# Finishing a two-step projection in the slot where it began, in an attention kernel paced by its exps

## The chip, the cores and the metric

One core of a Trainium2 chip. The metric is the device time of one execution in microseconds, the median over the runs of a kernel. Each run also records the mean clock that was granted to TensorE (1.000 is full speed). Ratios between kernels are the mean time of one kernel's fast runs over that of the other's fast runs of the same rounds, so they are not quite the ratio of the medians quoted beside them.

## The reference, cut to what matters

Two independent attention blocks on a sequence of 2048 with 32 heads of 16 columns, their outputs side by side:

```python
def _A_ref(x, wqkv, wo):          # every query sees every key
    ...
    p = _softmax(jnp.einsum("bhqd,bhkd->bhqk", q, k) * (Dh ** -0.5), axis=-1)
    o = jnp.einsum("bhqk,bhkd->bhqd", p, v)
    return (...o...) @ wo
def _B_ref(x, wqkv, wo):          # as A, with a causal window of 256
    mask = (idx[:, None] - idx[None, :] >= 0) & (idx[:, None] - idx[None, :] < W)
    ...
return jnp.concatenate([a, b], axis=-1)
```

Block A alone needs 32 x 2048 x 2048 exps. These set the time.

## The kernel before

The kernel is a scheduler. It cuts the work into 731 slots. A slot is one exp of up to three score tiles of 128 x 512 on ScalarE (some slots hold narrower ones, of block B, so that there are 747 exps), and round it the scheduler emits TensorE's work: scores of the slot after next, values of finished exps, and at the end of the slot at most a little other work. Two buffers of three PSUM banks hold scores ("sps"), one bank holds values ("op"), and a single bank ("ms") serves everything else: projections (k, q, v, output, and "padded" ones for the first heads), some guards, and a share of the exps that VectorE computes with a polynomial (steps "d").

A projection needs four matmuls. It is cut into two steps of two, and the bank is open between them:

```python
    def busy(self, bank, n):                       # warm-up: result never used
        for _ in range(n):
            self.nc.tensor.matmul(bank, lhsT=self.ident[:], rhs=self.junk, start=True, stop=True)
    ...
    def pair(self, first, second):
        def f():
            self.open = self.bank()
            first(self.open[:])                    # two matmuls
        def g():
            bank, self.open = self.open, None
            self.closed = self.slot
            second(bank[:])                        # two matmuls, then VectorE's copy
        return [f, g]
    ...
    def scores(self, slot):
        ...
            if b == 0 and jb.inst == 0:
                self.busy(sps[:, 0, :], 2 - self.whole)   # ahead of the scores
    ...
    def fill(self, s, tasks, done):
        if self.open is None:
            if self.closed == s or not self.by(self.freed, 0.9):
                return False
            ...                                    # pick the next task that may run
        ...
        self.whole += (kind in "kqop") * 2 + (kind in "dv")
        t["steps"].pop(0)()
        ...
    # end of each slot in run():
            self.whole = 0
            ...                                    # a guard or a step "d", if the bank is free
            must = self.open is not None           # a pair begun in the last slot
            while ((credit >= (CROWD if full else 1.0) or must)
                   and self.fill(s, tasks, done)):
                credit -= 1.0
                must = False
                if full:
                    break
```

`credit` grows with the urgency of the tasks; `CROWD` is 3.0. So a pair normally takes two slots, and one slot only if there was credit for two steps. `full` marks a slot whose coming scores all have a mask. `whole` counts how much work the slot gave to TensorE; a slot with less than 2 gets warm-up matmuls ("fillers" below) ahead of the next scores of block A.

Of the kernel before, what the change touches and what calls it, by code (L numbers as in the profile page):

```python
# [114 lines left out]
class _Kernel:  # L115
# [900 lines left out]
    def run(self):  # L1016
        done = set(self.start())
        self.vec = self.freed = self.op_free = 0.0
        slots, self.pend = self.slots()
        self.poly_pend = {key: list(groups) for key, groups in self.poly.items()}  # L1020
        tasks = self.plan(slots, done)
        polys = [t for t in tasks if t["name"][0] == "d"]
        tasks = self.tasks = [t for t in tasks if t["name"][0] != "d"]
        credit = poly_credit = 0.0
        for n in range(2):
            self.whole = n - 1
            self.scores(slots[n])
        self.whole = 2
        for s, sl in enumerate(slots):
            self.slot = s  # L1030
            self.exps(sl)
            if s == 2:
                self.more_constants()
                self.load_wo(0)
            if self.dq and self.by(self.vec, 0.6):
                self.queued(1.22, at=0)
                self.dq.pop(0)()
            if s + 2 < len(slots):
                self.scores(slots[s + 2])
            elif s + 1 == len(slots):  # L1040
                self.mid, finish = self.last_out(0, NPASS - 1)
            self.values()
            due = [x for x in self.later if x[0] <= s]
            self.later = [x for x in self.later if x[0] > s]
            for _, f in due:
                f()
            credit = min(credit + min(self.rate(s, tasks), 2.5), 3.0)
            poly_credit = min(poly_credit + self.rate(s, polys), 3.0)
            self.whole = 0
            if (self.guards and self.guards[0][0] <= s and self.open is None  # L1050
                    and self.by(self.freed, 0.9)):
                self.guards.pop(0)[1]()
                self.closed = s
                self.whole = 1
            full = s + 2 < len(slots) and all(jb.blocks for jb in slots[s + 2]["jobs"])
            if (poly_credit >= (2.5 if full else 1.0) and self.open is None
                    and self.fill(s, polys, done)):
                poly_credit -= 1.0
            must = self.open is not None
            while ((credit >= (CROWD if full else 1.0) or must)  # L1060
                   and self.fill(s, tasks, done)):
                credit -= 1.0
                must = False
                if full:
                    break
        while self.pend:
            self.slot += 1
            if self.dq:
                self.dq.pop(0)()
            self.values()  # L1070
            assert self.slot < len(slots) + 30, (self.dq, polys, self.poly_pend)
        assert not tasks + polys and not self.guards, [t["name"] for t in tasks]
        for _, f in sorted(self.later, key=lambda x: x[0]):
            f()
        finish()
# [49 lines left out]
```

## Time and profile before

| | before |
|---|---|
| median of the first 4 runs (the prediction starts from 1030.4, the median of the three known by then) | 1029.65 us (1028.13 to 1030.47) |
| ScalarE busy | 993.7 us, 97% of the span |
| TensorE busy | 918.5 us, 89% |
| wide exps (128 x 1536) | 705, 957.8 us |
| lateness of the wide exps | 25.2 us |
| fillers | 613 |

"Lateness" is used throughout. It is worked out from the trace: for each wide exp, the distance from the end of the exp before it to its own end, less 1.343 us, the distance that most of them keep; then summed. It is what ScalarE loses when scores come late. The lines that carry this are in the prediction.

### The profile page before, as it was taken

Reading aid. Unit: us, or ns where it says so; the run is one execution under the profiler, and the core shown is the slowest. Engines: PE = TensorE matmul, PEld = TensorE weight load, DVE = VectorE, ACT = ScalarE, POOL = GpSimd, SP = SyncE. Lnnn points to the kernel's source line nnn. Section 1 sums busy time; section 2 is a strip of 40 time slices with the busy share of each in tenths; the row PEclk is TensorE's granted clock in tenths of the full one; section 3 lists DMA queues with packets and bytes.
Section 4 is the critical chain, followed back from the end, with each engine's and each line's share of the span. In section 5 each row is a group of like instructions: output and inputs, shape, how many; then the busy total and the mean of one; then the engine's idle time right before and its main releaser. Section 6 shows DMA issues by size and latency. Waiting matters only on the chain.

```text
span 1027.8 us, 18725 instructions
## 1 busy us (share of the span) xinstructions
PE 918.5 (89%) x7577; PEld 314.1 (31%) x7658; DVE 804.2 (78%) x1032; ACT 993.7 (97%) x763; POOL 20.0 (2%) x100
## 2 busy tenths in 40 slices
PE   7999889899888998988899899899998998998887
PEld 5322222232223322332323332233332333233322
DVE  4532279887968898788888898988898878988874
ACT  5999999989999999999999999999999999999996
POOL 6000000000000000000000000000000000000000
PEclk9999999989999999999999999999999999999999
DMA  7021431212232102221240213123202221230011
GB/s 247 8 81 38 144 111 46 76 61 64 74 88 76 64 21 92 79 74 38 74 117 21 74 63 96 58 75 90 79 20 82 74 90 45 60 107 27 32 34 42
DMA packets 72359, 73.05 MB, mean 71 GB/s; under 512 B 22584, under 2 KB 55888, under 8 KB 72272
## 3 DMA queue, kind: packets, MB, share of 16 engines
q1 hardware_dynamic: 69216, 68.01, 21.4%
q0 software_dynamic: 768, 2.13, 0.5%
q10 hardware_dynamic: 2288, 1.70, 0.5%
q8 instruction: 60, 0.98, 0.4%
q14 instruction: 27, 0.22, 0.1%
HBM read 38.65 MB, written 31.07 MB: 68 GB/s over the span
## 4 chain that ended last, share of the span: by engine, by line
ACT 52%; PE 22%; DVE 14%; issue 10%; DMA 2%; ACTq 0%; DVEq 0%
ACT pT L599 52%; PE sps L572 5%; PE ms L252 4%; PE op L691 4%; PE sps L156 4%; DVE dy L631 3%; DVE dh L642 3%; DVE dh L646 2%; PE sps L581 2%; PE ms L628 2%; DVE pD L652 1%; DMA kTa<-in_A_x_dram 1%; DVE ob L421 1%; DVE osb L772 1%; DMA wk<-in_B_wqkv_dram 1%
## 5 line engine op out<-in xcount | busy, mean ns | idle before, releaser
L599 ACT ACTIVATE pT<-sps 128x1536 bf16<-128x1536 f32 (+2 forms) x747 | 983.6, 1465 | 15.4 <-PE sps L572 10.5
L156 PE MATMUL sps<-ident 128*128 128x512 bf16 x613 | 206.8, 382 | 46.6 <-ACT pT L599 39.1
L572 PE MATMUL sps<-qTa,kTa 32*128 32x512 bf16 (+1 forms) x1868 | 242.8, 378 | 5.8 <-ACT pT L599 0.7
L631 DVE COPY dy<-ms 128x512 f32<-128x512 f32 x240 | 164.2, 684 | 63.2 <-PE ms L628 61.3
L691 PE MATMUL op<-pT,va 128*32 128x512 bf16 (+1 forms) x1868 | 182.3, 382 | 0.0
L642 DVE SCALAR_TENSOR_TENSOR dh<-dy 128x1024 f32<-128x1024 uint16 x120 | 146.4, 1220 | 2.7
L646 DVE SCALAR_TENSOR_TENSOR dh<-dy,dh 128x1024 f32<-128x1024 uint16 x120 | 146.1, 1218 | 1.5
L652 DVE SCALAR_TENSOR_TENSOR pD<-dh,dy 128x1024 uint16<-128x1024 f32 x120 | 145.7, 1214 | 1.1
L572 PEld LDWEIGHTS <-kTa 32*128 32x128 bf16 x1868 | 61.1, 91 | 224.6 <-issue 223.7
L156 PEld LDWEIGHTS <-ident 128*128 128x128 bf16 x613 | 56.4, 96 | 162.0 <-issue 150.4
L628 PE MATMUL ms<-qTa,kTa 32*128 32x512 bf16 (+1 forms) x244 | 91.5, 378 | 14.1 <-DVE ob L421 3.8
L691 PEld LDWEIGHTS <-va 128*32 128x32 bf16 x2112 | 50.0, 93 | 102.1 <-issue 100.7
L581 PE MATMUL sps<-mask,ident 128*128 128x128 bf16 (+1 forms) x640 | 77.8, 248 | 0.0
L572 PE MATMUL sps<-qTb,kTb 32*128 32x384 bf16 (+2 forms) x704 | 58.2, 274 | 13.2 <-ACT pT L599 10.8
L581 PEld LDWEIGHTS <-ident 128*128 128x128 bf16 x640 | 43.4, 97 | 32.2 <-issue 29.8
L772 DVE COPY osb<-op 128x512 f32<-128x512 f32 x62 | 42.6, 687 | 8.2 <-PE op L691 7.8
L270 DVE CAST kst<-ms 128x512 bf16<-128x512 f32 x28 | 19.2, 686 | 33.0 <-PE ms L252 33.0
L345 DVE CAST va<-ms 128x368 bf16<-128x368 f32 (+1 forms) x28 | 11.8, 441 | 34.7 <-PE ms L252 34.7
L252 PE MATMUL ms<-wv,xT 128*128 128x368 bf16 (+2 forms) x163 | 35.2, 313 | 3.4 <-DVE dy L631 1.8
L572 PEld LDWEIGHTS <-kTb 32*128 32x128 bf16 x704 | 25.0, 92 | 38.6 <-issue 35.0
L628 PEld LDWEIGHTS <-kTa 32*128 32x128 bf16 x244 | 22.0, 91 | 47.4 <-issue 46.6
L252 PE MATMUL ms<-xT,wq 128*128 128x512 bf16 x100 | 32.2, 388 | 4.0 <-DVE dy L631 1.6
(106 smaller groups left out, 440.2 us busy)
## 6 DMA issues: line engine op xcount, KB each, us to landing
od<-osb SPq DMA_DIRECT2D x62, 256.0 KB
oc<-od SPq DMA_DIRECT2D x31, 256.0 KB
rb<-rd SPq DMA_DIRECT2D x31, 256.0 KB
kTb<-kd SPq DMA_DIRECT2D x16, 256.0 KB
qTb<-qd SPq DMA_DIRECT2D x16, 256.0 KB
qd<-qs SPq DMA_DIRECT2D x31, 128.0 KB
out_dram<-ob SPq DMA_DIRECT2D x31, 128.0 KB
qTa<-qd SPq DMA_DIRECT2D x15, 256.0 KB
```

What stands on the lines that cost most here:

```text
L156: self.nc.tensor.matmul(bank, lhsT=self.ident[:], rhs=self.junk, start=True, stop=True)
L252: self.nc.tensor.matmul(bank, lhsT=lhs(c), rhs=rhs(c), start=(c == 0), stop=(c == NC - 1))
L572: self.nc.tensor.matmul(sps[:, b, o:o + q1 - q0], lhsT=kT[r, gg, k0:k0 + P], rhs=qT[r, gg, q0:q1], start=(o == jb.subs[0][3]), stop=not jb ...
L581: self.nc.tensor.matmul(sps[:, b, o:o + P * len(kind)], lhsT=self.ident[:], rhs=m, start=False, stop=True, skip_group_check=True)
L599: nc.scalar.activation(out=pT[:, b:e, :n], in_=sps[:, b:e, :n], func=ACT.Exp, scale=LN2 / 128, bias=-127 * LN2)
L628: nc.tensor.matmul(b[:, o:o + q1 - q0], lhsT=kT[r, g % 2, k0:k0 + P], rhs=self.qT[0, p, g // 2][r, g % 2, q0:q1], start=True, stop=True, t ...
L631: nc.vector.tensor_copy(out=y[:, half, :], in_=b[:])
L642: nc.vector.scalar_tensor_tensor(out=st["h"][:], in0=low, scalar=-65536.0, in1=low, op0=ALU.add, op1=ALU.mult)
L646: nc.vector.scalar_tensor_tensor(out=st["h"][:], in0=low, scalar=65536.0 * POLY[1], in1=st["h"][:], op0=ALU.add, op1=ALU.mult)
L652: nc.vector.scalar_tensor_tensor(out=out.bitcast(U16), in0=st["h"][:], scalar=POLY[0] * 2.0 ** -41, in1=flat, op0=ALU.mult, op1=ALU.add)
L691: self.nc.tensor.matmul(op[32 * jb.j:32 * jb.j + 32, q0:q1], lhsT=self.v[jb.inst, kt][:, h * VP:h * VP + 32], rhs=jb.pT[:, o:o + q1 - q0], ...
L772: nc.vector.tensor_copy(out=osb[:], in_=self.op[i, p, g][:])
```

## The change

The intent: the single bank is held for one slot and not for two, so guards and VectorE's steps find it free more often. It is one line:

```diff
@@ end of each slot in run() @@
             while ((credit >= (CROWD if full else 1.0) or must)
                    and self.fill(s, tasks, done)):
                 credit -= 1.0
-                must = False
+                must = self.open is not None and not full
                 if full:
                     break
```

After a first step the bank is open, so the loop must take the second step in the same slot, unless the slot is `full`.

## The prediction

> **What bounds the kernel now.** I read the page first, then ScalarE's instructions kept apart by shape, then the table of waits, then the timeline of TensorE and of ScalarE around single slots.
>
> The page's head and its first group of costs:
>
> ```profile
> span 1027.8 us, 18725 instructions
> PE 918.5 (89%) x7577; PEld 314.1 (31%) x7658; DVE 804.2 (78%) x1032; ACT 993.7 (97%) x763; POOL 20.0 (2%) x100
> ...
> ACT 52%; PE 22%; DVE 14%; issue 10%; DMA 2%; ACTq 0%; DVEq 0%
> ...
> L599 ACT ACTIVATE pT<-sps 128x1536 bf16<-128x1536 f32 (+2 forms) x747 | 983.6, 1465 | 15.4 <-PE sps L572 10.5
> ```
>
> ScalarE is busy for 97% of the span, nearly all of it with the exps of line 599. They were idle for 15.4 us in total before them, 10.5 of it for the scores of line 572. So the kernel is ScalarE's chain of exps, and TensorE costs time only where scores come too late for the next exp.
>
> By shape, the wide exps are 705 of the 747. I took the distance from the end of each to the end of the exp before it. For 586 of the 705 it is within 0.02 us of 1.343 us: that is the pitch of a slot. The rest are longer, 25 us in sum, and this is what late scores cost. It is more than the 15.4 us of idle time shown, because an exp that starts late also loses its overlap with the one before: its record is about 1.47 us long against a pitch of 1.343. Hence the whole prize of any better order on TensorE is 25 us, 2.4% of the span, and most of that would have to be won for a "faster".
>
> The table of waits says who holds whom:
>
> ```profile
> DVE dy L631 <- PE ms L628: 61.3, 85, 3.4
> PE sps L156 <- ACT pT L599: 39.1, 112, 0.7
> PE sps L572 <- ACT pT L599: 11.5, 37, 0.8
> ACT pT L599 <- PE sps L572: 10.5, 28, 1.5
> PE ms L252 <- DVE dy L631: 8.0, 18, 0.8
> ```
>
> VectorE waits for TensorE (61.3 us for the scores of its own share of exps) and is no bound. TensorE waits for ScalarE in the slots with little work, where line 156 only keeps it warm. The single projection bank ("ms") costs TensorE 8.0 us of waiting for VectorE's copy out of it.
>
> **A pair in two slots and a pair in one.** Before the change both happen: 32 pairs already end in the slot where they begin (there was credit for two steps). So the trace holds the experiment already. First a pair over two slots, TensorE then ScalarE:
>
> ```profile
> 596.41 0.39 PE L572 MATMUL sps<-qTa,kTa 32*128 32x512 bf16 x3
> 596.94 0.59 PE L252 MATMUL ms<-wo,oTa 128*128 128x512 bf16 x2
> 597.47 0.39 PE L572 MATMUL sps<-qTa,kTa 32*128 32x512 bf16 x3
> 597.79 0.40 PE L691 MATMUL op<-pT,va 128*32 128x512 bf16 x4
> 598.12 0.60 PE L252 MATMUL ms<-wo,oTa 128*128 128x512 bf16 x2
> 598.66 0.39 PE L572 MATMUL sps<-qTa,kTa 32*128 32x512 bf16 x3
> ```
> ```profile
> 594.40 8.20 ACT L599 ACTIVATE pT<-sps 128x1536 bf16<-128x1536 f32 x6
> ```
>
> Two matmuls of a step take 0.53 us from the start of the step to the scores after them; six exps run without a gap. Then a pair in one slot:
>
> ```profile
> 585.47 0.39 PE L572 MATMUL sps<-qTa,kTa 32*128 32x512 bf16 x3
> 586.14 1.02 PE L252 MATMUL ms<-wo,oTa 128*128 128x512 bf16 x4 [0.28 <-DVE dy L631]
> 587.09 0.39 PE L572 MATMUL sps<-qTa,kTa 32*128 32x512 bf16 x3
> ```
> ```profile
> 587.59 5.61 ACT L599 ACTIVATE pT<-sps 128x1536 bf16<-128x1536 f32 x4 [0.17 <-PE sps L572]
> ```
>
> Scores to scores is 1.62 us here (585.47 to 587.09), over the pitch by 0.28. The exp that needs them starts 0.17 us late, and its end is 0.28 us late; the exp after it loses another 0.13.
>
> **What the Trainium skill says.**
> - "PSUM — Partial Sum Buffer", section "Engine vs sequencer instructions": matmuls start and complete in program order. So scores behind four projection matmuls can't overtake them. The timeline above agrees: the scores at 587.09 come after all four.
> - "ScalarE: Activation LUTs", section "What ACT_TABLE_LOAD costs": an ACTIVATE with immediate scale and bias takes 186 ns + 0.833 ns per column, and neighbours overlap by about 93 ns. For 1536 columns that is 1466 ns; the trace has about 1.47 us for an exp that starts late. The overlap here is larger, 1.47 - 1.343 = 0.13 us, and that is the figure I use: it is what each late start loses besides the wait itself.
> - "Perfetto Trace Analysis", section "Identifying the Most-Contended Engine": TensorE's busy share tells little of its headroom. I agree in use: the 89% includes 613 matmuls of line 156 that compute nothing, so I judge TensorE by how close its scores come to the exp, not by the share.
>
> **The change part by part.** It is one line of the scheduler: after the first step of a pair the second is now forced in the same slot, unless the slot issues scores with a mask in all its jobs. No matmul, copy, exp or DMA of the computation is added or removed; order is.
>
> I followed both kernels' schedulers slot by slot, 731 slots in each:
>
> | pair kind | one slot before | one slot after | newly in one slot |
> |---|---|---|---|
> | k | 6 | 28 | 22 |
> | q | 11 | 30 | 19 |
> | out | 9 | 29 | 20 |
> | padded first heads | 1 | 5 | 4 |
> | v | 5 | 32 | 27 |
>
> Added: warm-up matmuls. Each slot without work for TensorE puts up to two before the next scores; a pair in one slot covers only one slot, so its other slot is filled. TensorE's instruction order grows from 15,241 to 15,485 rows, 244 rows or 122 matmuls with their weight loads. At 0.27 us each (two take 0.54 from issue to the next scores, from 589.22 to 589.76 in this timeline) they are 33 us of TensorE time. They sit in slots that are otherwise nearly empty, where line 156 waits for ScalarE now, so I count nothing for them on the path.
>
> Moved: the second half of 92 pairs, one slot earlier. What that costs I take from the trace, for pairs whose neighbouring slots are all wide: the lateness of the third and fourth exp after the slot of the first step, mean in us over a 1.343 pitch, one slot against two.
> - k: 0.171 (6 pairs) against 0.033 (21): +0.138 x 22 = 3.0 us.
> - q: 0.162 (9) against 0.082 (17): +0.080 x 19 = 1.5 us.
> - out: 0.348 (7) against 0.052 (19): +0.296 x 20 = 5.9 us.
> - padded: 0.015 (1) against 0.004 (4): nothing.
> - v: 0.041 (5) against 0.063 (26): -0.022 x 27 = -0.6 us. Its matmuls are 144 or 368 columns wide, not 512.
>
> Sum +9.8 us.
>
> Taken off: about half of the pairs will be followed by an empty slot, where before nearly all had a step of VectorE's exps or another pair after them; there the fourth exp has time to recover, some 0.08 us for q and out. For about 25 pairs that is 2 us. And the bank is free sooner, so VectorE's exps are less often late: groups of values in bursts of 12 or more matmuls fall from 19 slots to 11, each worth some tenths. I take 1 us for these. Net +7 us.
>
> A second estimate from the same trace: I weighed each slot by its TensorE work, at the times read above, sorted the wide exps by how far the work of the one to three slots ahead of them exceeds the pitch, and took the mean lateness of each class. With the classes of the changed order this gives 32 us in place of 25: +7 again.
>
> **The rivals.**
> - The gain that the change seems meant for: the bank is held for one slot and not for two, VectorE's exps and the guards find it free, and their lateness goes. For: 8.0 us of waiting for the bank by line 252, and bursts of late values. Against: VectorE's 240 steps all have a slot today, and ScalarE waits for the scores of its own exps, not for VectorE. At best this gives 5 us back: 1025.
> - TensorE becomes the bound: 89% plus 33 us of warm-up matmuls is 92%, and every double slot is 0.3 to 0.4 us over the pitch. If warm-up matmuls do land ahead of scores that are already late, each of the 65 new doubles of k, q, out and the padded heads loses 0.35, as out does: 23 us, 1053.
> - Nothing: lateness falls into slots with slack. Scores mostly end 0.3 to 0.6 us ahead of the exp that needs them, and the q pairs show that a double slot can pass unseen (six of nine cost about 0.1 or less). Then 1031.
>
> **Range and chances.** Predicted 1037.5 us: 1030.4 plus 7. The low end, 1031, is the third rival with the first helping; the high end, 1046, is twice my cost per pair. Faster by over 2% would need 20.6 of the 25 us that exist: 1%. Slower by over 2% needs 1051, nearly the second rival in full: 5%. Within 2%: 94%.
>
> **What would show the steps right or wrong.**
> - ScalarE's busy time and number of exps stay (763 instructions). Its idle time before line 599 for the scores of line 572 should rise from 10.5 us to about 15, with more cases than 28; the excess of the wide exps over the 1.343 pitch from 25 to about 32.
> - Line 156 should have some 122 more matmuls; its waits for ScalarE should grow from 39.1 us, which says that they lie in slack. If they stay, the warm-up matmuls are on the path.
> - Late exps should sit two to three slots behind out and k pairs, not v pairs.
> - Waiting of line 252 for VectorE should fall or stay. If it rises, the single slot makes the bank the wait, and I'd be wrong about where the cost arises.
> - A time under 1029 would mean that lateness came mostly from the late bank; over 1046, that lateness piles up over several slots.

## The result, and the profile after

The changed kernel took 1043.90 us (1042.92 to 1048.24, 4 runs) against 1029.65, ratio 1.0148 with a 95% interval of 1.0117 to 1.0180. It is slower, by 14 us or 1.5% (less than the 2% that the prediction calls slower), and correct.

The page of the changed kernel, in the lines that answer to those shown of before:

```profile
span 1041.2 us, 19020 instructions
PE 942.3 (90%) x7702; PEld 327.3 (31%) x7780; DVE 802.5 (77%) x1032; ACT 998.4 (96%) x763; POOL 20.1 (2%) x100
...
ACT 55%; PE 24%; DVE 11%; issue 8%; DMA 2%; ACTq 0%; DVEq 0%
...
L599 ACT ACTIVATE pT<-sps 128x1536 bf16<-128x1536 f32 (+2 forms) x747 | 988.3, 1439 | 23.9 <-PE sps L572 14.4
L156 PE MATMUL sps<-ident 128*128 128x512 bf16 x735 | 239.2, 381 | 49.1 <-ACT pT L599 38.2
```

ScalarE does the same 763 instructions, and its idle time before the exps grew from 15.4 to 23.9 us. Fillers (line 156) grew from 613 to 735. The table of waits (who waited for whom, us in total, times, longest):

```profile
PE sps L156 <- ACT pT L599: 38.2, 113, 0.8
...
ACT pT L599 <- PE sps L572: 14.4, 41, 1.1
...
PE sps L572 <- ACT pT L599: 11.7, 35, 0.7
...
ACT pT L599 <- PE sps L581: 4.6, 13, 0.7
PE ms L252 <- DVE dy L631: 4.4, 14, 0.5
```

ScalarE waits for scores 41 times in place of 28. The projections wait less for the bank (4.4 us, not 8.0): the intent of the change was met, and it was worth little. The 122 fillers came without more waiting of line 156 for ScalarE (38.2 us, was 39.1). That is the first hint that they don't all lie in slack.

What it looks like on TensorE, where a k pair and a q pair follow one another (start, duration, engine, line, what; some matmul records are missing from a trace, here one of the four of the k pair):

```profile
824.69 0.39 PE L572 MATMUL sps<-qTa,kTa 32*128 32x512 bf16 x3
825.01 0.40 PE L691 MATMUL op<-pT,va 128*32 128x512 bf16 x4
825.34 1.04 PE L252 MATMUL ms<-xT,wk 128*128 128x512 bf16 x3
826.31 0.39 PE L572 MATMUL sps<-qTa,kTa 32*128 32x512 bf16 x3
826.63 0.40 PE L691 MATMUL op<-pT,va 128*32 128x512 bf16 x4
827.16 1.02 PE L252 MATMUL ms<-xT,wq 128*128 128x512 bf16 x4
828.12 0.39 PE L572 MATMUL sps<-qTa,kTa 32*128 32x512 bf16 x3
828.44 0.40 PE L691 MATMUL op<-pT,va 128*32 128x512 bf16 x4
828.77 0.61 PE L156 MATMUL sps<-ident 128*128 128x512 bf16 x2
```

and on ScalarE:

```profile
822.79 5.48 ACT L599 ACTIVATE pT<-sps 128x1536 bf16<-128x1536 f32 x4
828.62 4.13 ACT L599 ACTIVATE pT<-sps 128x1536 bf16<-128x1536 f32 x3 [0.35 <-PE sps L572]
```

From scores to scores it is 1.62 us and then 1.81, where ScalarE takes 1.343. The exp after the second pair starts 0.35 us late. After that TensorE, already behind, runs two fillers; these still fit, for the next scores follow at 829.31, 1.19 us after the last.

Where the time went: the last exp ends at 1032.7 us, before the change at 1019.3; the first exp and the tail are within 0.3 us of before. Lateness of the wide exps went from 25.2 to 38.0 us, and the narrower exps take 0.4 us more in all. So all of it is exps that end late, and nearly all of these waited for scores: the idle time before wide exps that ended with other work on TensorE (values, line 691) is 1.4 us, was 0.3.

**The granted clock.** One thing in the trace of before did not fit: its largest delay, 1.65 us, and two of 0.6 and 0.7 us sit together at 229 to 235 us. The view by stretches shows why (busy time and count of each engine, then the granted clock):

```profile
core 0: us, PE busy (x) PEld busy (x) DVE busy (x) ACT busy (x) POOL busy (x), PEclk, DMA share, GB/s
226.00:232.00 6.00, 5.78 (x28) 1.22 (x28) 4.46 (x8) 3.91 (x4) 0.00 (x0) 0.50 0.19 66
```

TensorE's clock was halved here for 6.8 us. That cost 3.6 of the 25.2 us of lateness. The trace of the changed kernel has no such stretch between its first and last exp. Hence at full clock the lateness went from 21.6 to 38.0, by 16 us.

Runs of one kernel differ by this clock. Over the 33 runs of the kernel before that went beside the experiments, a line through time against clock gives 1026.9 us at full clock and 0.68 us more per thousandth of clock lost; over the 8 runs of the changed kernel, 1041.8 and 0.75. So at full clock the change costs 14.9 us. Below, "at full clock" always means such a line through that kernel's own runs; it is an estimate, the better the nearer the runs came to 1.000. The experiments ran on three chips, and the kernel before on each of them; its lines for each chip alone give 1027.0 to 1027.1 us.

A second way needs no line. The exps come in the same order in all these kernels. So lateness can be summed over the same wide exps: those that lie outside the stretches of half clock, and the 5 us after each, in every trace compared. On 698 such exps it is 21.7 us before the change and 37.6 after, 16.0 us more. Below this is called "on the same exps". It holds for the profiled runs alone, one of each kernel.

### The profile page after: what moved, and what is told of

Its sections match the earlier page's. It is cut to its first block, busy times and chain, and to the rows that moved or that the text cites. A ratio compares the mean times of both kernels' runs of the same rounds, so it can differ in the third digit from the quotient of the medians.

```text
span 1041.2 us, 19020 instructions
## 1 busy us (share of the span) xinstructions
PE 942.3 (90%) x7702; PEld 327.3 (31%) x7780; DVE 802.5 (77%) x1032; ACT 998.4 (96%) x763; POOL 20.1 (2%) x100
## 4 chain that ended last, share of the span: by engine, by line
ACT 55%; PE 24%; DVE 11%; issue 8%; DMA 2%; ACTq 0%; DVEq 0%
ACT pT L599 55%; PE ms L252 6%; PE sps L572 5%; PE sps L156 5%; PE op L691 4%; DVE dy L631 3%; PE ms L628 2%; PE sps L581 2%; DVE dh L646 1%; DVE dh L642 1%; DVE pD L652 1%; DMA kTa<-in_A_x_dram 1%; DVE kst L270 1%; DVE osb L772 1%; DVE ob L421 1%
## 5 line engine op out<-in xcount | busy, mean ns | idle before, releaser
L599 ACT ACTIVATE pT<-sps 128x1536 bf16<-128x1536 f32 (+2 forms) x747 | 988.3, 1439 | 23.9 <-PE sps L572 14.4
L156 PE MATMUL sps<-ident 128*128 128x512 bf16 x735 | 239.2, 381 | 49.1 <-ACT pT L599 38.2
L156 PEld LDWEIGHTS <-ident 128*128 128x128 bf16 x735 | 65.2, 96 | 167.7 <-issue 157.0
L572 PE MATMUL sps<-qTb,kTb 32*128 32x384 bf16 (+2 forms) x704 | 58.1, 274 | 13.1 <-ACT pT L599 11.0
L581 PEld LDWEIGHTS <-ident 128*128 128x128 bf16 x640 | 43.4, 97 | 31.7 <-issue 29.3
L376 DVE TENSOR_SCALAR qs<-ms 128x512 bf16<-128x512 f32 x31 | 21.4, 690 | 21.0 <-PE ms L252 20.6
L572 PEld LDWEIGHTS <-kTb 32*128 32x128 bf16 x704 | 25.2, 92 | 37.6 <-issue 33.9
L691 PE MATMUL op<-pT,vb 128*32 128x384 bf16 (+2 forms) x704 | 36.0, 280 | 0.3 <-DVE osb L772 0.3
```

The source lines that it names most:

```text
L572: self.nc.tensor.matmul(sps[:, b, o:o + q1 - q0], lhsT=kT[r, gg, k0:k0 + P], rhs=qT[r, gg, q0:q1], start=(o == jb.subs[0][3]), stop=not jb ...
L581: self.nc.tensor.matmul(sps[:, b, o:o + P * len(kind)], lhsT=self.ident[:], rhs=m, start=False, stop=True, skip_group_check=True)
L599: nc.scalar.activation(out=pT[:, b:e, :n], in_=sps[:, b:e, :n], func=ACT.Exp, scale=LN2 / 128, bias=-127 * LN2)
L691: self.nc.tensor.matmul(op[32 * jb.j:32 * jb.j + 32, q0:q1], lhsT=self.v[jb.inst, kt][:, h * VP:h * VP + 32], rhs=jb.pT[:, o:o + q1 - q0], ...
```

## The experiments

Theory A: the four matmuls of a pair in one slot hold the next scores back, and fillers lie in slack. Theory B: the 122 added fillers are the cost. Theory C: it is the order on the bank and on VectorE, or any departure from a tuned order.

| run | fillers | median us | clock of its runs | ratio to before (95%) | at full clock |
|---|---|---|---|---|---|
| before (33 runs) | 613 | 1028.4 to 1030.4 | 0.988 to 0.999 | 1 | 1026.9 |
| changed (8 runs) | 735 | 1043.0, 1043.9 | 0.992 to 1.000 | 1.0138, 1.0148 | 1041.8 |
| e1 cover carried | 567 | 1051.4 | 0.971 to 0.990 | 1.0188 (1.0148 to 1.0227) | 1034.8 |
| e9 half carried | 656 | 1038.5 | 0.995 to 0.999 | 1.0102 (1.0089 to 1.0115) | 1037.6 |
| e2 only v pairs | 612 | 1032.8 | 0.993 to 0.998 | 1.0019 (1.0001 to 1.0037) | 1030.3 |
| e3 all but v | 740 | 1052.2 | 0.974 to 0.998 | 1.0186 (1.0159 to 1.0213) | 1044.6 |
| e4 fewer pairs | 592 | 1029.8 | 0.992 to 0.999 | 0.9987 (0.9965 to 1.0009) | 1026.6 |
| e5 halved, before | 613 | 1046.8 | 0.936 to 0.962 | 1.0073 (1.0030 to 1.0116) | 1010.9 (with its slow runs) |
| e6 halved, changed | 735 | 1025.7 | 0.989 to 0.994 | 0.9948 (0.9919 to 0.9978) | 1018.4 |
| e7 fillers in free bank, before | 613 | 1026.6 | 0.986 to 0.999 | 0.9978 (0.9943 to 1.0012) | 1024.8 |
| e8 fillers in free bank, changed | 735 | 1046.7 | 0.987 to 0.998 | 1.0173 (1.0140 to 1.0206) | 1043.8 |
| e11 fewer pairs + free bank | 592 | 1025.0 | 0.994 to 0.999 | 0.9968 (0.9955 to 0.9982) | 1023.7 |
| e12 e11 + cover carried | 566 | 1030.1 | 0.987 to 0.992 | 1.0017 (1.0004 to 1.0030) | 1023.0 |

All are correct but e5 and e6. One run of e3 and two of e5 were slow and are left out of the ratios; they are the low-clock end of their kernels or near it. (The slow run is also left out of the line for e3, but the line of e5 needs its two slow runs, since its two fast ones had nearly the same clock. The medians of e3 and e5, and the clocks in the table, are over all their runs.)

**e1: the fillers, with the order of the steps untouched.** The surplus of a slot with two steps counts as cover for the next slot too:

```diff
--- changed kernel
-            self.whole = 0
+            self.whole = max(0, self.whole - 2)
...
-                self.whole = 1
+                self.whole += 1
```

> The changed kernel with its order of steps untouched, but the surplus of a slot with two steps is counted as cover for the next slot too, so the next slots get no warm-up matmuls for it (168 fewer than in the changed kernel, 46 fewer than before the change). Theory A (the four projection matmuls themselves hold the scores back, warm-up matmuls lie in slack): 1040 to 1043 us against 1044, only the fourth exp after a pair gains. Theory B (the 122 added warm-up matmuls are the cost): back to 1030 to 1033 us, and the excess of the wide exps from 38 to about 26.

Measured 1042 to 1057 us: by the median slower than the changed kernel, and neither theory had this. But the clock of its runs was 0.971 to 0.990. The page of its profiled run (clock 0.990):

```profile
L599 ACT ACTIVATE pT<-sps 128x1536 bf16<-128x1536 f32 (+2 forms) x747 | 984.2, 1444 | 27.7 <-PE sps L572 19.5
...
L156 PE MATMUL sps<-ident 128*128 128x512 bf16 x567 | 187.5, 384 | 68.3 <-ACT pT L599 61.1
```

Its trace has four stretches at half clock between 569 and 880 us, each 3.4 us long. (A fifth, at 1026.6 us, catches the last exps.) With the exps of the four and the 5 us after each taken out, 28.8 us of lateness remain, against 38.0 in the changed kernel (no such stretch) and 21.6 in the kernel before. By the line through its runs it takes 1034.8 us at full clock. So at full clock taking 168 fillers out gives back 7 us of the 15; theory A's "in slack" is wrong for them. And theory B is wrong in that 8 us stay. The fillers also do what they are for: without them the clock falls, and that takes back more than they cost.

**e9: the same by half,** to see the cost at a clock near 1 and not by a line from afar:

```diff
--- changed kernel
-            self.whole = 0
+            self.whole = min(1, max(0, self.whole - 2))
...
-                self.whole = 1
+                self.whole += 1
```

> The changed kernel with only half of the surplus carried: 79 warm-up matmuls fewer than the changed kernel, 43 more than before the change. If warm-up matmuls cost by their TensorE time, whatever their place: halfway between the changed kernel and the run with all carried, at full clock 1038 us (1042 and 1035 are the ends), with a clock between theirs. If the run with all carried was fast for another reason: 1042 at full clock.

Three of its five runs had a clock of 0.999 and took 1038.0 to 1038.5 us; the changed kernel at 0.999 took 1042.7 and 1042.9. So 79 fillers fewer are worth 4.6 us at the same clock (the difference of the means), near halfway as expected. This needs no extrapolation. Per filler it is 0.058 us (4.6/79), a fifth of the 0.27 us that one takes on TensorE.

This mean hides two kinds. The two kernels differ in nothing but these 79 fillers, and following the scheduler slot by slot, as for the prediction, shows where they stand. 46 stand in empty slots right after a pair of k, q, output or padded heads: the 47 wide exps whose scores come next are late by 0.3 us in sum with them and by 0.0 without. The other 33 stand, one each, behind a step "d" in the slot right after a pair: the 36 wide exps whose scores come next are late by 4.3 us in the changed kernel and by 0.03 in e9. So 33 fillers cost 0.13 us each, which is the overlap that a late exp loses, and 46 cost next to nothing. (e1 agrees: of the 6.5 us that it is less late than the changed kernel on 679 of the same exps, 4.1 are in these slots.) One such slot, the changed kernel first, then e9; line 628 is the step "d":

```profile
787.47 0.39 PE L572 MATMUL sps<-qTa,kTa 32*128 32x512 bf16 x3
...
788.32 0.37 PE L628 MATMUL ms<-qTa,kTa 32*128 32x512 bf16 x1
788.62 0.39 PE L156 MATMUL sps<-ident 128*128 128x512 bf16 x1
788.94 0.39 PE L572 MATMUL sps<-qTa,kTa 32*128 32x512 bf16 x3
```
```profile
787.96 4.27 ACT L599 ACTIVATE pT<-sps 128x1536 bf16<-128x1536 f32 x3 [0.17 <-PE sps L572]
```
```profile
784.10 0.39 PE L572 MATMUL sps<-qTa,kTa 32*128 32x512 bf16 x3
...
784.95 0.37 PE L628 MATMUL ms<-qTa,kTa 32*128 32x512 bf16 x1
784.96 0.58 PE L572 MATMUL sps<-qTa,kTa 32*128 32x512 bf16 x3
```
```profile
784.60 4.13 ACT L599 ACTIVATE pT<-sps 128x1536 bf16<-128x1536 f32 x3 [0.18 <-PE sps L572]
```

The pair makes the first of the three exps late in both. From these scores to the next it is 1.47 us with the filler and 0.86 without, and the three exps take 4.27 us and 4.13.

**e10: the changed kernel again,** on the same chip as e9:

> The changed kernel once more, beside the others on this chip, to have its times against the clock of each run: 1042 us at full clock and about 0.7 us more for each thousandth of clock lost, by all theories.

Measured 1043.01 us (1042.17 to 1043.75), the fastest at a clock of 1.000. As expected at full clock; the clock spread of 0.003 is too small to test the slope by itself (these four runs alone give 0.45). With the first four runs the slope is 0.75 us per thousandth.

**e2 and e3: which pairs.**

```diff
--- changed kernel, e2 (e3 has != in place of ==)
-                must = self.open is not None and not full
+                must = self.open is not None and not full and self.cur["name"][0] == "v"
```

> The second step is forced into the same slot for v pairs only (32 v pairs in one slot, the others as before the change: 22 of k, q, out and padded). Theory A: 1029 to 1031 us, v pairs being narrow and their third exp losing 0.1 at most. Theory C (any departure from the tuned order costs, through the bank and the order on VectorE): 30% of the moved pairs, 30% of the 14 us: 1034.

Measured 1032.8 us, between the two theories. At full clock it is 3.4 us over the kernel before, though v pairs were expected to be free. In its trace the four exps from the second to the fifth after a v pair in one slot are 0.129 us late in sum (31 pairs); in the kernel before it is 0.070 for v pairs over two slots (26). Over 27 moved pairs that is 1.6 us of the 3.4; the rest I can't place.

> The second step is forced for all pairs but v (28 k, 31 q, 28 out, 5 padded in one slot). Theory A: nearly the whole loss, 1042 to 1044 us. Theory C: 70% of it, 1040.

Measured 1046.4 to 1052.4 us in its fast runs, above both theories, and above the changed kernel with all pairs forced. Part is clock (0.991 to 0.998). By its line e3 is still 2.8 us over the changed kernel at full clock, and the two halves, 3.4 and 17.7 us, add to 21.1 and not to 14.9. But the trace doesn't bear this out. Two stretches of half clock fall among its exps, 13.7 us from 154 us on and 3.4 us at 922; the 13 wide exps in and just after them are 10.0 us late, and 1.6 us in the changed kernel. That is half of the time at half clock, more than the line assumes. On 691 of the same exps e3 is late by 36.9 us and the changed kernel by 36.4. On the 679 that can be compared in all four kernels lateness is 19.5 us before, 22.3 in e2, 35.2 in e3 and 35.8 in the changed kernel: the halves cost 2.8 and 15.7, the whole 16.3. So the wide pairs (k, q, output) carry nearly all of the loss, and that forcing v pairs too makes it smaller is not shown. Theory C in its simple form (each moved pair costs alike) has both halves wrong: 30% of the pairs cost 2.8 of 16.3, the other 70% nearly all.

**e4: the other way, fewer pairs in one slot.**

```diff
--- kernel before
                 must = False
-                if full:
+                if full or self.open is not None and credit < 1.5:
                     break
```

> The opposite of the change, on the kernel before it: after a first step the second is taken in the same slot only with a credit of 1.5 or more, not 1.0; pairs of k, q and out in one slot fall from 26 to 14. Theory A: 12 pairs at about 0.3 us each, 3 us faster than before the change: 1026 to 1028. Theory C: the order before is tuned and this one is not: 1030 to 1035.

Measured 1029.8 us, ratio 0.9987 (0.9965 to 1.0009): the same. The expected 3 us are not there, at most 0.2 at full clock, and on 693 of the same exps lateness is equal (20.0 us). Between 14 and 26 such pairs of k, q and output (and with 21 fillers fewer) the kernel doesn't care, where 92 more pairs, v and padded ones included, cost 15 us.

**e5 and e6: is it the length on TensorE, or the order?** In both kernels one matmul per step in place of two. The changed kernel keeps its order of steps, copies, exps and DMAs, but a pair in one slot is now as long as one step was.

```diff
--- kernel before (e5), changed kernel (e6)
     def proj_mm(self, bank, lhs, rhs, cs):
+        if len(cs) == 2:
+            cs = [c for c in cs if c in (0, NC - 1)]
         for c in cs:
```

> The kernel before the change with one matmul per projection step in place of two (wrong result on purpose, control for the next run). All theories: somewhat faster than before, 1018 to 1026 us, the granted clock perhaps lower.

> The changed kernel with one matmul per projection step (wrong result on purpose); order, copies, exps and DMAs as in the changed kernel, so that a pair in one slot holds TensorE as long as one step did. Theory A (length of the lump on TensorE): within 4 us of the halved kernel before, at a like clock. Theory C (bank and order on VectorE): 10 us or more slower than it.

With less work on TensorE the clock fell so far that e5 became slower than the kernel before: 1036.8 and 1039.3 us in its two fast runs (clock 0.962 and 0.961), more in its two slow ones. The changed order has 122 more fillers and kept 0.989 to 0.994; so e6, at 1025.7, beats e5, and it beats the kernel before as well. By the lines they would be 7.5 us apart at full clock (1010.9 and 1018.4), but the line of e5 rests on its slow runs and reaches over 0.04 of clock, so it decides nothing.

The traces do better. On 626 of the same exps (in all four kernels) lateness is 10.0 us in e5 and 13.4 in e6, 3.4 apart; in the kernel before and the changed one it is 19.0 and 32.1, 13.1 apart. That is theory A's "within 4" and not theory C's 10 or more. Where the lateness goes also fits: on the 84 wide exps whose scores come right behind a pair of k, q, output or padded heads it is 20.2 us in the changed kernel and 3.7 in e6, whose order and fillers are the same. So the length of these pairs on TensorE holds most of the loss. (e6 also has less TensorE work in all; these runs do not split that from the length.)

**e7 and e8: do the fillers cost because of where they stand?** A filler ahead of scores writes to the scores' banks and so waits for the exp that frees them. Here they go into the projection bank at the slot's end where that is free, in the same number:

```diff
--- kernel before (e7), changed kernel (e8)
                 if full:
                     break
+            if (s + 3 < len(slots) and slots[s + 3]["jobs"][0].inst == 0 and self.whole < 2
+                    and self.open is None and self.by(self.freed, 0.9)):
+                self.busy(self.bank()[:], 2 - self.whole)
+                self.whole = 2
```

> The kernel before with the same number of warm-up matmuls, but those of a slot whose projection bank is free go into that bank at the slot's end, and no longer wait for the exp that frees the scores' banks. Theory B' (warm-up matmuls stand ahead of scores after that wait and are part of the lateness): 1020 to 1027 us, line 156 waits for ScalarE 10 to 25 us in place of 39. Theory A (they lie in slack): 1029 to 1031.

> The same edit on the changed kernel: all its 122 added warm-up matmuls kept, most of them out of the way of the scores. Theory B': 1033 to 1038 us, as the run with carried cover would have at full clock, and the clock at 0.995 or more. Theory A: 1042 to 1044.

In e8 more than half the fillers moved, and their wait for ScalarE fell from 38.2 to 21.1 us:

```profile
L156 PE MATMUL ms<-ident 128*128 128x512 bf16 x410 | 122.8, 381 | 19.7 <-DVE dy L631 8.7
...
L156 PE MATMUL sps<-ident 128*128 128x512 bf16 x325 | 116.8, 383 | 24.4 <-ACT pT L599 21.1
```

but the time did not fall: 1046.7 us, 1043.8 at full clock. The fillers in the new place now wait for VectorE (8.7 us). This does not show that the place is indifferent, for the edit left the costly ones where they were: all 410 moved fillers are of empty slots, and the 33 behind a step "d" right after a pair (see e9) still stand ahead of the scores. The 36 exps behind those are 3.8 us late, was 4.3. The 200 wide exps behind empty slots that follow a step "d" or a pair, where fillers cost little, are 5.2 us late and were 1.4. In the kernel before the same edit gave 2.1 us at full clock (1024.8) and nothing that the interval of the ratio would call a gain.

**e11 and e12: a version faster than both.**

```diff
--- kernel before (e11); e12 adds the carry of e1
                 must = False
-                if full:
+                if full or self.open is not None and credit < 1.5:
                     break
+            if (s + 3 < len(slots) and slots[s + 3]["jobs"][0].inst == 0 and self.whole < 2
+                    and self.open is None and self.by(self.freed, 0.9)):
+                self.busy(self.bank()[:], 2 - self.whole)
+                self.whole = 2
```

> Candidate for faster than both: fewer pairs in one slot (credit of 1.5) and warm-up matmuls into the projection bank where it is free. If the two small gains add: 1024 us at full clock, 1024 to 1027 measured, ratio to before 0.996. If each was noise: 1029 to 1030.

Measured 1025.0 us against 1028.4 of the kernel before in the same rounds, ratio 0.9968 (0.9955 to 0.9982): faster than both kernels, by a small but resolved margin (0.3%).

> The same with the surplus cover carried too (47 warm-up matmuls fewer than before the change): at full clock 2 us under the run without it, 1022, by TensorE's time; measured 1023 to 1028, since the clock may be granted less.

Measured 1030.1 us: slower than e11 by 5. By the lines it would be 0.7 us faster at full clock (1023.0), which is less than a line through clocks of 0.987 to 0.992 can tell; on 680 of the same exps the two are late by 17.1 and 17.2 us. The clock of its runs is 0.008 lower on average, with 26 fillers fewer. This repeats e1 in small on another order.

## Why the prediction was right or wrong, point by point

- *ScalarE's chain of exps bounds the kernel, and TensorE costs only where scores are late.* Right: busy time and number of exps stayed, the ends of the kernel stayed, and the whole loss is lateness. The direction and "within 2%" were right. The size was not: 7 us predicted, 14 measured, 14.9 at full clock. The high end of the range, 1046 us, was set as twice the pairs' cost; a good part of the miss came from the fillers instead, so that 1043.9 still lies inside is in part luck.
- *"They sit in slots that are otherwise nearly empty ... so I count nothing for them on the path."* This is the step that failed. The count of 122 was right. At full clock 168 fillers cost 7 us (changed kernel against e1, which has also some of the old ones less), and 79 of them 4.6 us at a like clock (e9). The profile after showed it as the prediction said it would: their wait for ScalarE did not grow. The flaw in the reasoning is in the words "otherwise nearly empty". For the 46 of e9 in empty slots it was right: they cost 0.3 us of lateness. But 33 stand behind a step "d" in the slot right after a pair, where TensorE is behind already, and cost 4.2 us.
- *The pairs themselves, +9.8 us less 3.* Near what stays when the fillers are gone: e1 is 8 us over the kernel before at full clock. But e1 has 46 fillers fewer than the kernel before, so the pairs' own cost may be a little higher. That it is the pairs' length on TensorE is shown by e6. The terms were all low when read in the changed kernel, fillers included: lateness of the third and fourth exp was 0.310 for k (0.171 predicted from), 0.268 for q (0.162), 0.410 for output (0.348), 0.279 for the padded heads (0.015) and 0.099 for v (0.041). In e1, outside its stretches of half clock, k, q, output and padded are at 0.219, 0.217, 0.305 and 0.060. The 23 k, q, output and padded pairs (neighbouring slots all wide) that the kernel before had in one slot were a milder sample: from scores to scores they took 1.675 us and the 83 of the changed kernel 1.727, and the third exp was 0.149 late against 0.241. The pair that the prediction shows in one slot (1.62 us) was no clean sample either: 0.28 us of it is a wait for the bank.
- *Half of the pairs are followed by an empty slot, where the fourth exp recovers.* Right: with an empty slot next, the fourth exp is 0.007 us late on average (44 pairs), with a step of VectorE's exps next 0.120 (32), nearly all of it the filler behind that step (see e9). Not foreseen: seven pairs are followed at once by another pair, where it is about 0.46 or more on average, as in the timeline above.
- *v pairs cost nothing.* Wrong by a little: 3.4 us at full clock in e2.
- *The bank is free sooner.* Right as a mechanism (the wait of line 252 for VectorE's copy 8.0 to 4.4 us). What it gained was not measured by itself.
- *The second estimate, by TensorE's work per slot, +7.* It counted the fillers' work, but took the mean lateness of classes in which few slots followed a pair, and missed as much as the first.
- *The rivals.* "TensorE becomes the bound" had the mechanism that the prediction left out, fillers ahead of scores that are already late, but not its size. The gain by the freed bank is not what the time shows. "Nothing" failed too: lateness grew by 12.8 us.
- *What the prediction did not see at all:* that 3.6 of the 25 us of lateness came from a stretch of half clock, and that the clock falls when many fillers are taken out (0.971 to 0.990 in e1). This also bounds the prize of a better order: of the 25 us, 21.6 were to be had.

## What to carry to other kernels

An engine that is off the critical path has slack per slot, not on average. Moving work between two slots at an unchanged total can cost what exceeds the slot, and filler work that is harmless in an empty slot (46 fillers, 0.3 us) is on the path where other work and a late start have used the slot up (33 fillers, 4.2 us). Before you count filler work as free, take half of it out and look, at a like clock, and look in which slots the time came back. And print the granted clock beside each time: here 0.02 of clock is 14 us, as much as the whole change, and the run that removed fillers looked like a failure until its times were set against it.

## What the Trainium skill lacked or had wrong

- "TensorE: Matmul & The Clock Gate", Part 1 (and its table of goals): the page lets the clock halve after an idle window of about 3.4 us, and warns of idle gaps over about 3 us. Its section "A second HAM failure mode: psum-queue depth-cycling" has a clock that goes back and forth because TensorE idles briefly and often, but gives no length. Here it halved with brief gaps alone. In e1 it halved at 569.2 us; in the 7 us before, the longest idle gap of TensorE was 0.69 us, and in the 3.4 us before, TensorE was busy for 2.36 us of 3.40. The view by stretches of e1, the stretch before and the stretch of half clock:

```profile
565.80:569.20 3.40, 2.36 (x18) 0.67 (x17) 2.90 (x7) 3.40 (x3) 0.00 (x0) 1.00 0.14 39
```
```profile
569.20:572.60 3.40, 3.40 (x15) 0.75 (x14) 2.43 (x3) 1.85 (x3) 0.00 (x0) 0.51 0.01 2
```

  Nine such stretches between 150 and 930 us in the traces of before, e1, e3 and e11 begin after a longest gap of 0.34 to 2.28 us. They last 3.41 us, or two or four times that, which agrees with the page's window. Their factor is 0.5 each time, as the page has it. What share of a window must be busy, no page says and these runs do not settle.
- The same page has no price for it in a kernel paced by another engine. Here it is 0.68 us of time per thousandth of mean clock over 33 runs. A thousandth less of mean clock is about 2 us spent at half clock (2 x 0.001 x 1028), so about a third of a stretch at half clock is lost. Single traces show more: 3.2 us for 6.8 in the kernel before and 8.4 for 17.1 in e3, each against the same exps of the changed kernel.
- "ScalarE: Activation LUTs", "What ACT_TABLE_LOAD costs": neighbouring exps overlap by about 0.13 us here (1.47 us alone, 1.343 us apart), not 93 ns; the duration of a single one agrees (1466 ns by the page).
- "Perfetto Trace Analysis", "Identifying the Most-Contended Engine": that TensorE's busy share is a poor measure holds, 89% and 90% for kernels 15 us apart. No page says how to tell whether fillers lie on the path; the run e9, 79 fewer for 4.6 us, is one way, and comparing the same exps slot by slot tells which ones.
